# Attention backward: transposed softmax rows are made where they are used and moved inside SBUF, and ScalarE issues them and the dV stores

## The chip, the cores and the metric

The kernel runs on one core of one Trainium2 chip. The metric is the device time of one execution in microseconds, lower is better; the median over runs of the same kernel is compared.

## The reference, cut to what matters

One token goes through an adaLN block: attention against a cache of 32 heads x 8192 keys x 192, then a small gated mixer and MLP. The kernel returns the output and eight gradients. The bulk is the gradients of the two caches.

```
def _A_ref(x, k_cache, v_cache, wq, wo):          # B = Sq = 1, 32 heads, Sk = 8192, Dh = 192
    q = (x @ wq).reshape(B, Sq, Hq, Dh).transpose(0, 2, 1, 3)
    scores = einsum('bhqd,bhkd->bhqk', q, k) * Dh ** (-0.5)
    p = softmax(scores)
    o = einsum('bhqk,bhkd->bhqd', p, v)
    return o.transpose(...).reshape(B, Sq, Hq * Dh) @ wo
...
_out, _vjp = jax.vjp(_f, A_x, A_k_cache, A_v_cache, A_wq, A_wo, B_w3, B_w4, c, w_mod)
return (_out, *_vjp(grad_out))
```

With e = exp(score - max) and do the gradient at the attention output of a head, dV[k, :] = e[k] / sum(e) * do, an outer product, and dK[k, :] = ds[k] * q with ds made from V . do. So every byte of K and of V is read, V is read a second time, and every byte of dK and dV is written, all in bf16.

## The kernel before, in words

A head's 8192 keys lie as 128 partitions x 64 columns (J = 64); a half is 32 columns (JH), 1.5 MB of K or V. E_all keeps e of all heads, column j of head h at E_all[:, h, j].

**Forward** (lines 509 to 598, then an ending written out by hand for the last two heads). Per head, SyncE (SP) loads two halves of K and two of V. VectorE (DVE) multiplies K by q, TensorE (PE) sums over the 192 columns, ScalarE (ACT) takes exp, and PE accumulates three sums over the keys. For each pair of heads, e_rows transposes the pair's 128 columns of E_all on PE, e_rows_out copies the result from PSUM on ScalarE, and GpSimd (POOL) stores it to eT_d, a scratch tensor in DRAM (line 431). There are 16 such pairs.

**Middle.** The mixer, the MLP and their backward, on single columns: a long chain of small operations. From line 777 on the backward's pools are open. do_mm makes do of the last heads (ScalarE writes do_r at line 839), and load_er fetches the first two halves' rows of e.

**Backward** (lines 1234 to 1285). 64 stages, one per half head, last heads first. A stage s does this:

- DVE: pq = V * do in two quarters (mul_q, L936); PE sums it over the columns (tree_q, L945); DVE reduces (L313) and makes dS4 (L1242).
- DVE writes dK in two parts (dk_part, L961); POOL stores it (store, L1194).
- dV: eight groups of four PE matmuls of depth 1 (dv_groups, L956). A weight is one row of 128 values of e, taken from er_b, which has its rows on partitions 0, 32, 64 and 96. ScalarE copies each group from PSUM (L957). Two PSUM buffers (psV) and two er_b buffers are in turn. After the eighth group, POOL issues load_er for stage s + 2 (L801), then the store of dV (L1194).
- SP loads the V half of a later stage (L293).
- slot() puts in pieces of the weight gradients (g_do, g_dq, g_wm, g_dwo): they load wq, w_mod and wo, transpose them on PE and store dwq, dw_mod and dwo.

The order on PE, DVE, ScalarE and SP is the order in which the code writes the operations (manual_schedule with ORDER)[...]. V halves have three buffers. dV and dK take five buffers in turn (out_b): dV of stage s is number 2s, dK is 2s + 1, so dK of stage s overwrites what dV of stage s - 2 left, and dV of stage s what dK of stage s - 3 left.

dv() says how many dV groups stand at a place. The eighth of a stage stands at the end of the stage, before the second part of dK in the text of the program.

Of the kernel before, what the change touches and what calls it, by code (L numbers as in the profile page):

```python
# [8 lines left out]
FP32 = mybir.dt.float32  # L9
BF16 = mybir.dt.bfloat16  # L10
ALU = mybir.AluOpType
# [9 lines left out]
def kernel(  # L21
# [26 lines left out]
    nc = tc.nc  # L48
    P = 128
    D = A_x.shape[-1]  # L50
    _, HQ, S, DH = A_k_cache.shape
# [3 lines left out]
    J = S // P  # L55
    JH = J // 2
# [4 lines left out]
    NQ = QD // P  # L61
    NMB = NMOD // P
    NT = HQ // 2
# [3 lines left out]
    MW = DH + 1  # L67
# [5 lines left out]
    V_, A_, T_ = nc.vector, nc.scalar, nc.tensor  # L73

    const = ctx.enter_context(tc.tile_pool(name="const", bufs=1))
# [6 lines left out]
    psB = ctx.enter_context(tc.tile_pool(name="psB", bufs=1, space=PS))  # L82
    psS = ctx.enter_context(tc.tile_pool(name="psS", bufs=1, space=PS))

    ORDER = {mybir.EngineType.PE, mybir.EngineType.DVE, mybir.EngineType.Activation, mybir.EngineType.SP}
    dram = ctx.enter_context(tc.tile_pool(name="dram", bufs=1, space=bass.MemoryType.DRAM))


    A_.preload_act_table_set("natural_log_exp_and_others")
    ident_bf = const.tile([P, P], BF16, name="ident_bf")  # L90
# [21 lines left out]
    def col(n, name, dtype=FP32):  # L112
        return const.tile([P, n], dtype, name=name)
# [42 lines left out]
    def layernorm(x, name):  # L156
        res = []
        for _ in g_layernorm(x, name, res):
            pass
        return res[0]  # L160
# [41 lines left out]
    dV_hd = [out_3[0, h].rearrange("(p j) d -> p j d", p=P) for h in range(HQ)]  # L202
# [49 lines left out]
    n0, r0 = layernorm(x_c, "ln0")  # L252
# [18 lines left out]


    E_all = const.tile([P, HQ, J], BF16, name="E_all")
    M1 = const.tile([P, HQ, MW], FP32, name="M1")
    M2 = const.tile([P, NT, MW], FP32, name="M2")
    AO = const.tile([P, ND, HQ], FP32, name="AO")
    rinv = col(HQ, "rinv")
    o_col = col(NQ, "o_col")
# [33 lines left out]
    def dot_sum(ps, dst):  # L312
        V_.reduce_sum(out=dst, in_=ps, axis=AX.X)  # L313

    eT_d = dram.tile([HQ * J, P], BF16, name="eT_d")
    NKB = 5
    KB = [kp.tile([P, JH, DH], BF16, name=f"KB{b}") for b in range(NKB)]

# [1 line left out]
    H1 = HQ - 1  # L320
    TL = NT - 1
# [2 lines left out]
    OR = (KY, KC, KE, KX, KD)  # L324
    NVA = (7 * JQ) // 16
    MO = 256
    with tc.tile_pool(name="vs", bufs=3) as vsp, tc.tile_pool(name="ft", bufs=2) as ft, \
            tc.tile_pool(name="psM", bufs=2, space=PS) as psM, tc.tile_pool(name="psO", bufs=2, space=PS) as psO, \
            tc.tile_pool(name="psR", bufs=2, space=PS) as psR:
# [36 lines left out]
        def m_units(q, kb, vs, mp, last=3):  # L366
# [7 lines left out]
            def rest():  # L374
                for k in range(JQ):
                    p0 = 64 * (k % 2)
                    T_.matmul(mp[p0 : p0 + 64, MO : MO + MW], lhsT=kb[:, j0 + k, P:DH], rhs=vs[:, k, 0:MW], start=False, stop=(z and k >= JQ - 2), skip_group_check=True)  # L377

# [28 lines left out]
        def mp_out(h, mp):  # L407
            A_.copy(out=M1[:, h, :], in_=mp[:, 0:MW])
            mt = ft.tile([P, MW], FP32, name="mt", bufs=1)
            A_.copy(out=mt[64:128, :], in_=mp[64:128, MO : MO + MW])  # L410
            return mt
# [7 lines left out]
        def m_add(h, mp, mt):  # L419
            t, b = divmod(h, 2)  # L420
            V_.tensor_tensor(out=M2[64 * b : 64 * b + 64, t, :], in0=mp[0:64, MO : MO + MW], in1=mt[64:128, :], op=ALU.add)

        def e_rows(t, pool=psS, tag="s"):
            ps = pool.tile([P, P], BF16, name="er_ps", tag=tag)
            T_.transpose(out=ps[0 : 2 * J, :], in_=E_all[:, 2 * t : 2 * t + 2, :].rearrange("p h j -> p (h j)"), identity=ident_bf)
            return ps

        def e_rows_out(t, ps):
            er = ft.tile([P, P], BF16, name="er", bufs=1)
            A_.copy(out=er[0 : 2 * J, :], in_=ps[0 : 2 * J, :])  # L430
            nc.gpsimd.dma_start(out=eT_d[2 * t * J : (2 * t + 2) * J, :], in_=er[0 : 2 * J, :])

        def pair_sum(po, b, os_h):
            rows = slice(64 * b, 64 * b + 64)
            for k in range(3):
                T_.matmul(po[rows, k : k + 1], lhsT=os_h[:, k:DH:3], rhs=c32[:, 0:1], start=True, stop=True)
            T_.matmul(po[rows, 3:4], lhsT=c32[:, 0:64], rhs=os_h[:, DH:MW], start=True, stop=True)
            T_.matmul(po[:, 4 + b : 5 + b], lhsT=c32, rhs=os_h[:, DH:MW], start=True, stop=True)
# [27 lines left out]
        X, os_, wo_l = {0: {"k": [load_k(0, 0), load_k(0, 1)], "v": [load_v(0, 0, VB[0])]}}, {}, {}  # L466
        wo_l[0] = load_wo(0)
        wch = None
        V_.memset(M1[:, H1 - 1 : HQ, :], 0.0)
        V_.memset(M2[:, TL, :], 0.0)  # L470
        dgs = list(range(NF))
        w4v = B_w4.rearrange("(a p) r -> p a r", p=P)
        a1, nga, sS, sS2, C_S, S_m = col(ND, "a1"), col(ND, "nga"), col(ND, "sS"), col(ND, "sS2"), col(1, "C_S"), col(1, "S_m")
# [35 lines left out]
        with tc.manual_schedule(engines=ORDER):  # L509
            for i in range(H1):  # L510
# [5 lines left out]
                t = (i - 3) // 2  # L516
# [44 lines left out]
                    vs = scale_v(2, y["v"][1], E4, Ef)  # L561
                if last:
                    A_.copy(out=AO[:, :, 2 * t : 2 * t + 2], in_=pair_ao(o2, wo_l.pop(t)))
                    e_rows_out(t, e_rows(t))
                if i % 4 == 3 and wch is not None:
                    q_half((i + 1) // 4, 1, wch)
                    wch = None
# [77 lines left out]
            score_tree(1, d0)  # L645
            o_quarter(3, z["vs"], z["op"])
            mt = m_out(H1 - 2, z["mp"], z["op"], os_)
            e_rows_out(TL - 1, e_rows(TL - 1, psB, "b"))
            es = e_sum(H1 - 1)
            dg_part(1)  # L650
            op_y = psO.tile([P, 256], FP32, name="op")
# [43 lines left out]
            pair_sum(po, 1, os_.pop(H1 - 2))  # L695
            o2 = pair_o(TL - 1, po)
            pair_sum(po_x, 1, os_.pop(H1))
            e_rows_out(TL, e_rows(TL, psB, "b"))
            ps_ao = pair_ao(o2, wo_l[TL - 1])
            w3t(1)  # L700
            o2 = pair_o(TL, po_x)
# [13 lines left out]
            ps = mean_mm(x1, ND)  # L715
# [8 lines left out]
            ps = mean_mm(pr, 2 * ND)  # L724
# [9 lines left out]
            ps = mean_mm(pr, 2 * ND)  # L734
# [48 lines left out]
    cpr = col(HQ, "cpr")  # L783
    ckS = col(NQ, "ckS")
# [9 lines left out]
    NS = 2 * HQ  # L794

    def load_er(s):

        er = bst.tile([P, R8, P], BF16, name="er_b", bufs=2)
        h, t = ht(s)
        r0 = h * J + t * JH  # L800
        nc.gpsimd.dma_start(out=er[0:P:32, :, :].rearrange("r k p -> r (k p)"), in_=eT_d[r0 : r0 + JH, :].rearrange("(r k) p -> r (k p)", r=4))  # L801
        return er

    def ht(s):
# [115 lines left out]
    def late_rows():  # L920
        V_.tensor_tensor(out=bo, in0=h2_ps, in1=xc2, op=ALU.add)
        dw4_rows(flat(VB[0])[:, 2 * D :], 5, 7)
        dw4_store(flat(VB[0]), 3, 9)
        v_l[2] = load_v(*ht(2), VB[0])
        dw4_rows(stg0, 0, 3)
        dw4_store(stg0, 0, 3)
        hm = col(1, "hm")
        V_.tensor_scalar(out=hm, in0=vt[:, 1:2], scalar1=r1[:, 0:1], scalar2=S_m[:, 0:1], op0=ALU.mult, op1=ALU.add)
        V_.tensor_scalar(out=bo, in0=bo, scalar1=hm[:, 0:1], scalar2=None, op0=ALU.add)
        V_.tensor_tensor(out=ao, in0=aoP, in1=aoN, op=ALU.add)  # L930
        V_.memset(dha, 0.0)
        V_.memset(dsc, 0.0)
        V_.memset(dq_x, 0.0)

    def mul_q(s, q):
        V_.tensor_tensor(  # L936
# [121 lines left out]
    def g_dq(t):  # L1058
# [6 lines left out]
        else:  # L1065
            for lo, hi, M, b in ((0, P, M1[:, 2 * t, 0:DH], 0), (0, P, M1[:, 2 * t + 1, 0:DH], 2), (0, 64, M2[0:64, t, 0:DH], 1), (64, P, M2[64:128, t, 0:DH], 1)):
                h = 2 * t + (1 if (b == 2 or lo == 64) else 0)
# [19 lines left out]
    def g_small():  # L1087

        ck3 = ckS.rearrange("p (t b) -> p t b", b=3)
        for b, h0 in ((0, 0), (2, 1)):  # L1090
            V_.tensor_tensor(out=ck3[:, :, b], in0=M1[:, h0:HQ:2, DH], in1=cpr[:, h0:HQ:2], op=ALU.mult)
        for lo, hi, h0 in ((0, 64, 0), (64, P, 1)):
            V_.tensor_tensor(out=ck3[lo:hi, :, 1], in0=M2[lo:hi, :, DH], in1=cpr[lo:hi, h0:HQ:2], op=ALU.mult)
        A_.mul(out=ckS, in_=ckS, mul=SCALE)
        V_.tensor_tensor(out=d_cb, in0=d_sb, in1=n1, op=ALU.mult)
        V_.tensor_tensor(out=d_ga, in0=dx1, in1=ao, op=ALU.mult)
        yield
        V_.tensor_tensor(out=d_gb, in0=bo, in1=dy_c, op=ALU.mult)
        x2 = tcol(ND, "x2")
        V_.tensor_tensor(out=x2, in0=bo, in1=gb, op=ALU.mult)  # L1100
        V_.tensor_tensor(out=x2, in0=x2, in1=x1, op=ALU.add)
        store_vec(x2, out_0[0], "x2")
        yield
# [87 lines left out]

    def store(dst, s, src, lo=0, hi=JH):
        h, t = ht(s)
        nc.gpsimd.dma_start(out=dst[h][:, t * JH + lo : t * JH + hi, :], in_=src[:, lo:hi, :])  # L1194

    def dv_gen():
        for s in range(NS):
            dV, er, doh = out_b(2 * s), er_l.pop(s), do_of(ht(s)[0])
            for n, g in enumerate((0, 2, 4, 6, 1, 3, 5, 7)):
                dv_groups(dV, er, doh, (g,))  # L1200
                if n == 7:
                    if s + 2 < NS:
                        er_l[s + 2] = load_er(s + 2)
                    store(dV_hd, s, dV, JQ if s == 0 else 0, JH)
                elif n == 3 and s == 0:
                    store(dV_hd, s, dV, 0, JQ)
                yield
# [7 lines left out]
    ps = psR.tile([P, JH, TS], FP32, name="dot_ps")  # L1215
# [18 lines left out]
    for s in range(NS):  # L1234
        h, t = ht(s)
# [7 lines left out]
            out=dS4,  # L1243
            in0=dP[:, :, None].to_broadcast([P, JH, 4]),
            scalar=cpr[:, h : h + 1],
            in1=E_all[:, h, t * JH : (t + 1) * JH, None].to_broadcast([P, JH, 4]),
# [8 lines left out]
        if nxt:  # L1255
            ps = psR.tile([P, JH, TS], FP32, name="dot_ps")
# [59 lines left out]
```

## Time and profile before

| | |
|---|---|
| Median of 14 runs | 1445.3 us (1441.19 to 1454.22) |
| The profiled execution, its own time | 1450.06 us |
| Its span | 1448.3 us |
| Busy in the span: PE, DVE, ACT, POOL | 1186.0, 1111.2, 882.2, 143.6 us |
| Moved by DMA | 572.48 MB, 395 GB/s on the mean |
| DMA queue of SP (hardware) | 51402 packets, 343.59 MB, 59.1% of 16 engines |
| DMA queue of POOL (software) | 26704 packets, 226.97 MB, 37.9% |
| DMA queue of ScalarE (hardware) | 20 packets, 0.00 MB |
| Granted TensorE clock | 0.73 over the span, about 0.57 in the backward |

Busy time is that of the engine's own instructions; a DMA is issued by one engine and carried out by the 16 DMA engines, whose busy share is told per stretch of time. "A <- B" in a wait means that A stood idle until B was done. The profiled execution is 4.8 us above the median, so differences are worked out on the profile and then set against the median.

### The profile page before, as it was taken

To read this page: it belongs to the slowest core of one execution; us is meant where nothing else is said; L and a number is where in the kernel's file an instruction comes from. 1 tells how busy PE (TensorE), PEld (TensorE's weight loads), DVE (VectorE), ACT (ScalarE), POOL (GpSimd) and SP (SyncE) were. 2 spreads that over 40 slices of the span, in tenths; PEclk is the share of its full clock that TensorE was granted. 3 is DMA by queue.
4 is the path that set the end of the run, shared out by engine and by line. 5 is a ranking of instruction groups with operands and counts; after the bars stand their busy time and mean duration, and the time that the engine had idled before them with its cause. 6 is when DMAs were issued, how large, how long until landed. Compare 5 with 4: busy or idle time off the path is not lost.

```text
span 1448.3 us, 29985 instructions
## 1 busy us (share of the span) xinstructions
PE 1186.0 (82%) x12577; PEld 776.9 (54%) x12577; DVE 1111.2 (77%) x1396; ACT 882.2 (61%) x1923; POOL 143.6 (10%) x256
## 2 busy tenths in 40 slices
PE   3999999899999998777788777778788887677974
PEld 1677777677777677544444444444444444344532
DVE  5999999999999997577666666667766667677674
ACT  0777767777777773545556555656656565455654
POOL 0000000000000000112111111111111011011111
PEclk9999999999999997756555655565555556655555
DMA  9999999999999996599999999999999999999997
GB/s 375 399 408 417 414 418 402 399 403 402 398 392 397 414 387 259 206 361 426 423 426 418 416 396 392 420 417 401 402 418 415 418 419 412 390 379 416 419 408 330
DMA packets 78261, 572.48 MB, mean 395 GB/s; under 512 B 8846, under 2 KB 26974, under 8 KB 37806
## 3 DMA queue, kind: packets, MB, share of 16 engines
q1 hardware_dynamic: 51402, 343.59, 59.1%
q0 software_dynamic: 26704, 226.97, 37.9%
q8 instruction: 98, 1.61, 0.4%
q14 instruction: 37, 0.30, 0.1%
q10 hardware_dynamic: 20, 0.00, 0.0%
HBM read 344.10 MB, written 226.43 MB: 394 GB/s over the span
## 4 chain that ended last, share of the span: by engine, by line
PE 36%; DVE 27%; DMA 14%; ACT 11%; issue 10%; POOL 1%; SPq 0%; POOLq 0%; ACTq 0%; DVEq 0%
PE dot_ps L945 14%; DVE prod L298 8%; DMA out_dram<-KB 7%; DVE pq L936 5%; PE dv_ps L956 5%; ACT vs L357 4%; PE mp L372 3%; DVE prod L303 3%; DVE vs L350 3%; PE wT_ps L824 3%; PE dot_ps L309 3%; PE mp L377 2%; ACT wT L825 2%; ACT KB L957 2%; DMA KB<-in_A_k_cache_dram 2%
## 5 line engine op out<-in xcount | busy, mean ns | idle before, releaser
L957 ACT CAST KB<-dv_ps 128x768 bf16<-128x768 f32 x504 | 382.0, 804 | 284.9 <-PE dv_ps L956 284.0
L945 PE MATMUL dot_ps<-pq,ident_bf 128*128 128x256 bf16 x1536 | 355.1, 400 | 76.1 <-DVE pq L936 75.9
L357 ACT ACTIVATE vs<-VB,Ef 128x192 bf16<-128x192 bf16 x840 | 303.2, 443 | 0.0
L945 PEld LDWEIGHTS <-ident_bf 128*128 128x128 bf16 x1536 | 186.9, 132 | 199.3 <-issue 139.6
L956 PE MATMUL dv_ps<-do_r,er_b 1*128 1x192 bf16 x2048 | 215.8, 328 | 64.1 <-ACT KB L957 55.1
L961 DVE TENSOR_TENSOR KB<-qs_bc,dS 128x3072 bf16<-128x3072 bf16 x126 | 220.6, 1751 | 44.0 <-DMA out_dram<-KB 38.9
L936 DVE TENSOR_TENSOR pq<-VB,do_r 128x3072 bf16<-128x3072 bf16 x126 | 220.5, 1750 | 6.2 <-DMA VB<-in_A_v_cache_dram 6.2
L298 DVE TENSOR_TENSOR prod<-KB,qs_bc 128x6144 bf16<-128x6144 bf16 x62 | 207.8, 3352 | 13.0 <-DMA KB<-in_A_k_cache_dram 6.9
L956 PEld LDWEIGHTS <-er_b 1*128 1x128 bf16 x2048 | 90.2, 110 | 182.1 <-issue 170.0
L372 PE MATMUL mp<-vs,KB 128*128 128x193 bf16 x1920 | 187.7, 251 | 0.0
L372 PEld LDWEIGHTS <-KB 128*128 128x128 bf16 x1920 | 168.6, 100 | 18.7 <-issue 4.6
L313 DVE TENSOR_REDUCE dP<-dot_ps 128x32 f32<-128x512 f32 x64 | 44.2, 691 | 127.6 <-PE dot_ps L945 127.6
L309 PE MATMUL dot_ps<-prod,ident_bf 128*128 128x512 bf16 x372 | 94.4, 391 | 42.1 <-DVE prod L303 42.1
L350 DVE TENSOR_TENSOR vs<-VB,E 128x1728 bf16<-128x1728 bf16 x120 | 123.5, 1049 | 0.0
L303 DVE TENSOR_TENSOR prod<-prod 128x3072 bf16<-128x3072 bf16 x62 | 108.6, 1751 | 0.6
L825 ACT COPY wT<-wT_ps 128x1024 bf16<-128x1024 bf16 x84 | 80.8, 962 | 42.0 <-PE wT_ps L824 40.5
L377 PE MATMUL mp<-vs,KB 128*64 128x193 bf16 x1920 | 104.2, 252 | 0.0
L801 POOL DMA_DIRECT2D er_b<-eT_d x64 | 37.0, 579 | 600.5 <-PE dv_ps L956 574.5
L377 PEld LDWEIGHTS <-KB 128*64 128x64 bf16 x1920 | 77.9, 110 | 19.7 <-issue 19.7
L309 PEld LDWEIGHTS <-ident_bf 128*128 128x128 bf16 x372 | 34.6, 99 | 83.6 <-issue 55.7
L1194 POOL DMA_DIRECT2D out_dram<-KB x127 | 68.5, 544 | 35.4 <-ACT KB L957 29.9
L337 ACT ACTIVATE E<-S_h,negm 128x256 bf16<-128x256 f32 x30 | 15.2, 508 | 82.0 <-DVE negm L532 82.0
(335 smaller groups left out, 1018.2 us busy)
## 6 DMA issues: line engine op xcount, KB each, us to landing
VB<-in_A_v_cache_dram SPq DMA_DIRECT2D x125, 1536.0 KB, 11.8
out_dram<-KB POOLq DMA_DIRECT2D x125, 1536.0 KB, 16.0
KB<-in_A_k_cache_dram SPq DMA_DIRECT2D x64, 1536.0 KB, 10.2
wo_st<-in_A_wo_dram SPq DMA_DIRECT2D x30, 480.0 KB, 8.4
w_st<-in_A_wq_dram SPq DMA_DIRECT2D x12, 960.0 KB, 13.8
out_dram<-wo_st POOLq DMA_DIRECT2D x16, 480.0 KB, 20.4
out_dram<-w_st POOLq DMA_DIRECT2D x7, 960.0 KB, 21.1
w_st<-in_w_mod_dram SPq DMA_DIRECT2D x6, 960.0 KB, 21.9
```

Of the source, the lines that this page charges most:

```text
L298: V_.tensor_tensor(out=prod, in0=src, in1=vec[:, None, :].to_broadcast([P, JH, DH]), op=ALU.mult)
L303: V_.tensor_tensor(out=prod[:, :, 0:w], in0=prod[:, :, 0:w], in1=prod[:, :, w : 2 * w], op=ALU.add)
L309: T_.matmul(ps, lhsT=ident_bf, rhs=prod[:, :, k : k + TS], start=(k == 0), stop=(k == w - TS))
L350: V_.tensor_tensor(out=vs[:, 0:n, 0:DH].rearrange("p j (a b) -> p j a b", b=4), in0=v[:, v0 : v0 + n, :].rearrange("p j (a b) -> p j a b", ...
L357: A_.activation(out=vs[:, k, 0:DH], in_=v[:, v0 + k, :], func=ACT.Copy, scale=Ef[:, j0 + k : j0 + k + 1])
L372: T_.matmul(mp[:, 0:MW], lhsT=kb[:, j0 + k, 0:P], rhs=vs[:, k, 0:MW], start=(q == 0 and k == 0), stop=(z and k == JQ - 1), skip_group_chec ...
L377: T_.matmul(mp[p0 : p0 + 64, MO : MO + MW], lhsT=kb[:, j0 + k, P:DH], rhs=vs[:, k, 0:MW], start=False, stop=(z and k >= JQ - 2), skip_grou ...
L936: V_.tensor_tensor(out=pq[:, q], in0=v_l[s][:, q * JQ : (q + 1) * JQ, :], in1=do_of(ht(s)[0])[:, None, :].to_broadcast([P, JQ, DH]), op=AL ...
L945: T_.matmul(ps[:, q * JQ : (q + 1) * JQ, :], lhsT=ident_bf, rhs=pq[:, q, :, k : k + TS], start=(k == 0), stop=(k == DH - TS), skip_group_c ...
L956: T_.matmul(ps[:, b, k * DH : (k + 1) * DH], lhsT=er[p0 : p0 + 1, 2 * m + k, :], rhs=doh[p0 : p0 + 1, :], start=True, stop=True)
L957: A_.copy(out=dV4[:, 2 * q : 2 * q + 2, m * PW : (m + 1) * PW], in_=ps[:, :, 0:PW])
L961: V_.tensor_tensor(out=dK[:, lo:hi, :].rearrange("p j (a b) -> p j a b", b=4), in0=qh.rearrange("p (a b) -> p a b", b=4)[:, None, :, :].to ...
```

## The change

The scratch tensor in DRAM goes. The forward makes no transposed rows any more, except those of the last pair, which stay in SBUF in er_t. In the backward, at the end of stages 2, 6, 10 up to 58, PE transposes the next pair's columns and ScalarE copies them into er_t, 15 times. load_er moves 32 rows of 128 values from er_t to er_b, SBUF to SBUF, and ScalarE issues it; ScalarE also issues the stores of dV. POOL keeps the stores of dK and of the weight gradients. M1, M2 lose the parts of the last two heads, which held zeros, and ckS is cleared there instead.

```
-    dram = ctx.enter_context(tc.tile_pool(name="dram", bufs=1, space=bass.MemoryType.DRAM))
+    erp = ctx.enter_context(tc.tile_pool(name="erp", bufs=1))
...
-    M1 = const.tile([P, HQ, MW], FP32, name="M1")
-    M2 = const.tile([P, NT, MW], FP32, name="M2")
+    M1 = const.tile([P, HQ - 2, MW], FP32, name="M1")
+    M2 = const.tile([P, NT - 1, MW], FP32, name="M2")
...
-    eT_d = dram.tile([HQ * J, P], BF16, name="eT_d")
...
+    def e_rows(t, pool=psS, tag="s"):
+        ps = pool.tile([P, P], BF16, name="er_ps", tag=tag)
+        T_.transpose(out=ps[0 : 2 * J, :], in_=E_all[:, 2 * t : 2 * t + 2, :].rearrange("p h j -> p (h j)"), identity=ident_bf)
+        er = erp.tile([P, P], BF16, name="er_t")
+        A_.copy(out=er[0 : 2 * J, :], in_=ps[0 : 2 * J, :])
+        return er
...
-        def e_rows_out(t, ps):
-            er = ft.tile([P, P], BF16, name="er", bufs=1)
-            A_.copy(out=er[0 : 2 * J, :], in_=ps[0 : 2 * J, :])
-            nc.gpsimd.dma_start(out=eT_d[2 * t * J : (2 * t + 2) * J, :], in_=er[0 : 2 * J, :])
...
-                    e_rows_out(t, e_rows(t))
...
-            e_rows_out(TL - 1, e_rows(TL - 1, psB, "b"))
...
-            e_rows_out(TL, e_rows(TL, psB, "b"))
+            er_t = [e_rows(TL, psB, "b")]
...
         er = bst.tile([P, R8, P], BF16, name="er_b", bufs=2)
         h, t = ht(s)
-        r0 = h * J + t * JH
-        nc.gpsimd.dma_start(out=er[0:P:32, :, :].rearrange("r k p -> r (k p)"), in_=eT_d[r0 : r0 + JH, :].rearrange("(r k) p -> r (k p)", r=4))
+        r0 = (h % 2) * J + t * JH
+        nc.scalar.dma_start(out=er[0:P:32, :, :], in_=er_t[0][r0 : r0 + JH, :])
         return er
...
     def store(dst, s, src, lo=0, hi=JH):
         h, t = ht(s)
-        nc.gpsimd.dma_start(out=dst[h][:, t * JH + lo : t * JH + hi, :], in_=src[:, lo:hi, :])
+        (nc.scalar if dst is dV_hd else nc.gpsimd).dma_start(out=dst[h][:, t * JH + lo : t * JH + hi, :], in_=src[:, lo:hi, :])
...
                 if n == 7:
+                    if s % 4 == 2 and s + 2 < NS:
+                        er_t[0] = e_rows(TL - s // 4 - 1)
                     if s + 2 < NS:
                         er_l[s + 2] = load_er(s + 2)
                     store(dV_hd, s, dV, JQ if s == 0 else 0, JH)
```

In the built program the order of every engine is otherwise the same. POOL issues 145 fewer DMAs (16 stores to eT_d, 64 loads of er_b, 65 stores of dV), and ScalarE 129 more.

More of the change, by code (lines that the diff above doesn't have):

```diff
@@ L421, in m_add @@
             V_.tensor_tensor(out=M2[64 * b : 64 * b + 64, t, :], in0=mp[0:64, MO : MO + MW], in1=mt[64:128, :], op=ALU.add)
[L423 to L426, printed above, removed]
-        def e_rows_out(t, ps):
-            er = ft.tile([P, P], BF16, name="er", bufs=1)
-            A_.copy(out=er[0 : 2 * J, :], in_=ps[0 : 2 * J, :])
-            nc.gpsimd.dma_start(out=eT_d[2 * t * J : (2 * t + 2) * J, :], in_=er[0 : 2 * J, :])
         def pair_sum(po, b, os_h):
@@ L468 @@
         wch = None
-        V_.memset(M1[:, H1 - 1 : HQ, :], 0.0)
-        V_.memset(M2[:, TL, :], 0.0)
         dgs = list(range(NF))
@@ L933, in late_rows @@
         V_.memset(dq_x, 0.0)
+        V_.memset(ckS[:, 3 * TL : NQ], 0.0)
     def mul_q(s, q):
@@ L1090, in g_small @@
         for b, h0 in ((0, 0), (2, 1)):
-            V_.tensor_tensor(out=ck3[:, :, b], in0=M1[:, h0:HQ:2, DH], in1=cpr[:, h0:HQ:2], op=ALU.mult)
+            V_.tensor_tensor(out=ck3[:, 0:TL, b], in0=M1[:, h0 : H1 - 1 : 2, DH], in1=cpr[:, h0 : H1 - 1 : 2], op=ALU.mult)
         for lo, hi, h0 in ((0, 64, 0), (64, P, 1)):
-            V_.tensor_tensor(out=ck3[lo:hi, :, 1], in0=M2[lo:hi, :, DH], in1=cpr[lo:hi, h0:HQ:2], op=ALU.mult)
+            V_.tensor_tensor(out=ck3[lo:hi, 0:TL, 1], in0=M2[lo:hi, :, DH], in1=cpr[lo:hi, h0 : H1 - 1 : 2], op=ALU.mult)
         A_.mul(out=ckS, in_=ckS, mul=SCALE)
```

## The prediction

> **What bounds the kernel now.** I read the page's slices first, then busy time by stretches, then the waits from 640 us on, then single tiles and the timeline at both ends of the backward.
>
> ```profile
> DMA  9999999999999996599999999999999999999997
> 20.00:560.00 540.00, 491.60 (x7031) 376.01 (x7034) 504.68 (x481) 376.89 (x1194) 8.26 (x15) 0.97 1.00 404
> 560.00:604.00 44.00, 33.13 (x497) 26.18 (x486) 31.70 (x118) 21.81 (x38) 6.01 (x9) 0.65 0.36 126
> 644.00:1396.00 752.00, 595.47 (x4509) 338.06 (x4508) 517.35 (x731) 436.57 (x616) 114.95 (x200) 0.57 1.00 411
> 1412.00:1432.00 20.00, 16.62 (x114) 8.43 (x113) 15.83 (x13) 12.99 (x18) 2.71 (x5) 0.50 0.78 324
> ```
>
> The columns are length, busy time of PE, PE loads, DVE, ACT and POOL, clock, DMA share, GB/s. The DMA engines are full, 1.00, in the forward and from 644 to 1396 us, while the busiest engine there, PE, has 79%. Only the middle (0.36) and the end (0.78) leave room: 28 us and 4 us. So time is won or lost in the middle, at the end, and by what changes the DMA engines' own work. A stall of an engine in the full stretch costs only what exceeds the cover. I size that cover from stages 59 to 61, where side work is over and loads are ending: POOL's er_b issues follow each other after 10.1 and 10.3 us, against 13.3 us a stage on the mean (55 stages from 667.7 to 1397.9 us). The side work's DVE rows (TENSOR_SCALAR of L1083, L1047 and L1051, reductions of L1069) come to about 1.5 us a stage and PE's (L824, L838, L1045) hold the trees up by about as much, not always at the same time; I take 1 us a stage to spare, a choice.
>
> ```profile
> POOL er_b L801 <- PE dv_ps L956: 567.7, 59, 17.8
> ACT KB L957 <- PE dv_ps L956: 272.8, 217, 5.5
> PE dv_ps L956 <- ACT KB L957: 54.4, 84, 1.5
> DVE KB L961 <- DMA out_dram<-KB: 38.9, 18, 8.8
> POOL out_dram L1194 <- ACT KB L957: 29.2, 58, 8.8
> PEld L956 <- DMA er_b<-eT_d: 9.0, 6, 4.2
> PE dv_ps L956 <- DMA er_b<-eT_d: 6.7, 3, 4.0
> ```
>
> Waits on transfers that the change touches: 38.9 us for stored buffers, 15.7 us for er_b. They end sooner after the change, but with the DMA engines full the time then shows as another wait for the same bytes.
>
> [...]
>
> **The change, part by part.**
>
> *Forward.* Out go 15 transposes and copies (217 and 267 ns, beside DMA) and 15 stores of 32 KB. Each is 16 packets of 2048 B[...], of 82 ns on the mean of POOL's packets of that size class: 15 x 0.08 = **-1.2 us** where DMA is full. Bounds -3 (the transposes also wait 3.6 us) and 0. The memsets and the shorter ckS products (under 1 us) lie beside the loads at the start and in the side work: 0; without that cover under 1 us.
>
> *Middle.* POOL issued the first two er_b loads at 580.6 and 581.2 and they landed at 584.4, well before PE needs them:
>
> ```profile
> 580.59 1.14 POOL L801 DMA_DIRECT2D er_b<-eT_d  x2 [16.32 <-PE w3T_ps L674]
> 587.88 0.42 ACT L839 ACTIVATE do_r<-do_ps,rinv 128x192 bf16<-128x192 f32 x1 [1.29 <-PE do_ps L838]
> 589.03 0.50 PE L956 MATMUL dv_ps<-do_r,er_b 1*128 1x192 bf16 x4
> ```
>
> On ScalarE they stand after L839, so they issue at about 588.3 and 588.7 (0.33 to 0.55 us each, SP's and ScalarE's rows). The quickest landing from the trace is 3 us (ScalarE's 1.36 us issue at the start of the kernel frees PE at 4.36): er_b is there at 591, and the first dv matmul moves from 589.0 by 2. Behind it in PE's order stand c_ps and the first tree, so the whole chain to the V load at 603.7 moves: **+1.9 us**, DMA being idle there. Bounds 0 (a shorter copy within SBUF) and +4.
>
> *Full stretch, DMA.* Bytes stay: 0.5 MB written and 0.5 MB read leave, 0.5 MB inside SBUF comes. The form changes. Each er_b load was 4 packets of 2048 B, 82 ns[...]. 256 B packets took 17 ns on ScalarE's queue at the start[...]. I take **+5 us**[...]. Bounds 0 and +9. The dV stores keep their 12288 B packets, most at 460 ns on both queues: 0, bounds -4 and +4.
>
> *Full stretch, engines.* ScalarE gains, per stage, two issues of 0.33 us and the wait for its own last copy, some 0.9 us, and every fourth stage a copy of 0.27 us behind a transpose of 0.22 us. Behind these stand the next stage's first copies; PE has two psV buffers, and a group takes PE 1.0 to 1.4 us against 0.8 us of copy, so PE goes on. Covered by the 1 us and by ScalarE's idle 42%; without cover 0.9 x 58 = 52 us. POOL no longer holds dK's store behind er_b and dV. A new wait comes with the queue[...]. I set the landings, where the trace tells them, against the POOL issues that ScalarE takes over: most waits have 8 to 25 us to spare, seven have under 3, four of them are late by 0.4 to 3.4 us, all on or behind a load of wq, w_mod or wo. Such loads are slow already:
>
> ```profile
> L985 SPq DMA_DIRECT2D stg<-in_A_wq_dram x4: 379/412/1171, 700.0 to 1198.6; - x4
> DMA to landing us min/median/max: 3.8/19.3/34.7
> ```
>
> [...] seven waits of 2 to 8 us, about 35 us in ScalarE, of which psV hides 2 to 3 us each. The rest fits the spare microsecond a stage; I take **+2 us**, bounds 0 and +15. The V halves keep their distance: 10 to 20 us before use in most stages, 2.2 and 2.6 at the least. [...] The copy into er_t waits for the last load from it, one stage old and landed after 8.5 us in the median (17.5 at the most, before): 0, up to +4 once where it is late, inside the +15.
>
> *End.* dK's store now leaves when DVE is done, not behind dV on POOL:
>
> ```profile
> 1423.55 1.75 DVE L961 TENSOR_TENSOR KB<-qs_bc,dS 128x3072 bf16<-128x3072 bf16 x1
> 1429.20 1.06 POOL L1194 DMA_DIRECT2D out_dram<-KB  x2 [8.80 <-ACT KB L957]
> 1434.98 1.06 POOL L1194 DMA_DIRECT2D out_dram<-KB  x2 [4.72 <-ACT KB L957]
> ```
>
> dK of stage 62 is ready at 1425.3 and leaves after 1429.7, while the DMA engines idle 22% of 20 us. Filling that saves up to 4.4 us; ScalarE's issues lengthen three uncovered stages by up to 0.6 us each. **-2.5 us**, bounds -4 and +1.
>
> Sum: -1.2 + 1.9 + 5 + 2 - 2.5 = +5.2 us. On the profiled 1450.06 that is 1455.3; on the median, 4.8 us lower, **1450.5**.
>
> **Rivals.** *Faster.* [...] the er_b copy lands within 1 us, the sum is -1.2 + 0 + 0 + 0 - 4 = -5: 1440. For it: dK's earlier store is sure, and er_b and dV each have a quieter queue. [...] *Much slower.* [...] 20 waits instead of seven, 5 us each, less 60 us of cover, plus V halves that come late: +15 to +25, 1460 to 1470. For it: 34.7 us for a load of wq[...]. [...] *Nothing to see.* DMA full before and after, ends cancel: 1445.
>
> **How the numbers follow.** A measurement of this kernel can tell about 0.2%, 3 us. My case (+1 to +10) gets 0.5, of which 0.15 fall within 0.2%; much slower 0.2; faster 0.2; nothing to see 0.1. That gives faster 0.20, same 0.25, slower 0.55. The range leaves out half of the faster case below -6 and the top of the slow one: 1439 to 1466; my case alone is 1446 to 1455.
>
> **What would show it.** Right: DMA share still 1.00 from 644 to 1396 us with GB/s a little lower (about 407); the first dv matmul later by 2 us against L839; dK's stores issued by POOL 3 us before dV's; waits for er_b near zero. A column of ScalarE waits on DMA, or DVE waits on V loads beyond 20 us, makes it the slow rival. Wrong: the full stretch shorter by 5 us or more, which would mean that the DMA engines were not the bound there.

## The result, and the profile after

The median went from 1444.8 us (48 runs) to 1467.93 us (10 runs, 1461.25 to 1472.21): ratio 1.0151, 95% interval 1.0131 to 1.0171, that is +21.8 us (18.9 to 24.7). The forecast was slower, at 1450.5; the time lies just above its range, 1439 to 1466.

The DMA row of the 40 slices on the changed kernel's page, and after it the busy times by stretches, with the columns used for the kernel before:

```profile
DMA  9999999999999994699999999999999999999997
```

```profile
20.00:560.00 540.00, 492.06 (x6988) 375.71 (x6987) 503.39 (x480) 372.75 (x1178) 0.00 (x0) 0.95 1.00 404
560.00:604.00 44.00, 32.53 (x453) 24.98 (x452) 29.27 (x118) 19.05 (x34) 1.96 (x2) 0.56 0.33 117
644.00:1396.00 752.00, 596.52 (x4454) 338.42 (x4452) 504.11 (x717) 432.79 (x619) 51.72 (x87) 0.55 1.00 403
```

The forward is as it was, 404 GB/s. The loss lies in the full stretch, from 644 to 1396 us: the DMA share still reads 1.00, but the engines move 403 GB/s instead of 411. The starts of DVE's reduction into dP, one per stage, tell where. Against before, stage 3 starts 4.1 us late, stage 60 23.6 us late, and the span ends 19.6 us late. So 19.5 us are lost over 57 stages, unevenly (the lag is 14.8 us at stage 16, 15.5 at stage 30, 20 at stage 39), and 4.0 us come back at the end. These are two single executions. What comes back at the end holds in the other runs too: from stage 60 on, the changed kernel, e2, e4, e6, e10 and e11, whose whole dV stores have left POOL, gain 2.5 to 4.8 us on the kernel before, and of those with them on POOL (e1, e3, e7, e9, e12) none gains more than 0.1 us.

The waits of the changed kernel from 640 us on (total us, times, longest):

```profile
ACT KB L950 <- PE dv_ps L949: 259.6, 233, 4.1
PE dv_ps L949 <- ACT KB L950: 77.3, 84, 2.7
DVE w_st L1040 <- ACT v_bc L1033: 42.4, 14, 5.0
DVE stg L1040 <- ACT v_bc L1033: 28.2, 12, 4.8
DVE KB L954 <- DMA out_dram<-KB: 19.4, 6, 4.2
ACT wT L817 <- DMA er_b<-er_t: 5.5, 13, 0.5
ACT KB L950 <- DMA er_b<-er_t: 1.9, 4, 0.5
POOL out_dram L1187 <- DVE KB L954: 208.3, 22, 15.5
```

Waits on transfers went down (DVE's for stored buffers from 38.9 to 19.4 us, PE's for er_b from 9.0 to nothing; the 15.7 us of the prediction count three waits twice, at a weight load and at the matmul behind it). Waits on ScalarE went up: PE for dV copies from 54.4 to 77.3, and DVE for v_bc, ScalarE's copy that feeds the rows of a weight gradient, from 50.5 to 70.6. The two lines of before:

```profile
DVE w_st L1047 <- ACT v_bc L1040: 30.1, 13, 3.9
DVE stg L1047 <- ACT v_bc L1040: 20.4, 11, 4.0
```

ScalarE itself hardly waits for DMAs (5.5 and 1.9 us above). POOL, with the dV stores gone, waits for DVE's dK (208.3 us) and stores it at once.

The end of stage 29, in the order of time, on ScalarE (ACTq is its sequencer, which issues the DMAs) in the changed kernel, from the timeline:

```profile
1017.56 0.80 ACT L950 CAST KB<-dv_ps 128x768 bf16<-128x768 f32 x1 [1.03 <-PE dv_ps L949]
1017.62 0.54 ACTq L793 DMA_DIRECT2D er_b<-er_t  x1
1018.39 0.44 ACTq L1187 DMA_DIRECT2D out_dram<-KB  x1
1019.00 2.20 ACT L950 CAST KB<-dv_ps 128x768 bf16<-128x768 f32 x3 [0.65 <-PE dv_ps L949]
```

In the kernel before, the same four copies follow each other without idle time, in one line of the view:

```profile
1001.93 2.93 ACT L957 CAST KB<-dv_ps 128x768 bf16<-128x768 f32 x4 [0.90 <-PE dv_ps L956]
```

This is the reading on which the rest turns. The er_b issue, 0.54 us, runs while the last dV copy computes. The dV store reads what that copy writes, so it is issued only at the copy's end (at 1018.39, the end being 1018.36; of the 65 dV stores none is issued earlier than 0.03 us after such an end), and ScalarE's next instruction starts 0.65 us after that end. I call this the **gap** and take its mean over stages 4 to 59, passing over the copy into er_t (and, below, unused copies): 0.82 us in the changed kernel, 0.11 in the kernel before. It can hold a wait for data too, so it is an upper mark, and the view names PE as what ended these 0.65 us. But no gap of these stages is under 0.40 us in the changed kernel, whatever follows, while the median before is -0.08 (the next copy starts just before the last one ends). Not every stage has more of it: at nine of them it was 0.37 us before already, with a wait for PE.

### The profile page after: what moved, and what is told of

Same layout as the page of the kernel before. It is cut to its first block, busy times and chain, and to the rows that moved or that the text cites. A ratio compares the mean times of both kernels' runs of the same rounds, so it can differ in the third digit from the quotient of the medians.

```text
span 1467.9 us, 29883 instructions
## 1 busy us (share of the span) xinstructions
PE 1210.8 (82%) x12577; PEld 788.1 (54%) x12577; DVE 1109.2 (76%) x1395; ACT 884.7 (60%) x1923; POOL 62.7 (4%) x111
## 3 DMA queue, kind: packets, MB, share of 16 engines
q8 instruction: 98, 1.61, 0.4%
## 4 chain that ended last, share of the span: by engine, by line
PE 45%; DVE 26%; ACT 14%; DMA 7%; issue 5%; ACTq 2%; SPq 0%; POOL 0%; DVEq 0%; POOLq 0%
PE dot_ps L938 21%; PE dv_ps L949 8%; DVE prod L297 8%; ACT vs L363 5%; ACT KB L950 4%; DVE pq L929 4%; DVE prod L302 3%; DVE vs L356 3%; PE mp L378 3%; PE wT_ps L816 3%; DMA KB<-in_A_k_cache_dram 2%; DMA out_dram<-KB 2%; PE dot_ps L308 2%; DVE S_h L312 2%; PE mp L383 2%
## 5 line engine op out<-in xcount | busy, mean ns | idle before, releaser
L938 PE MATMUL dot_ps<-pq,ident_bf 128*128 128x256 bf16 x1536 | 365.6, 409 | 44.8 <-DVE pq L929 44.7
L949 PE MATMUL dv_ps<-do_r,er_b 1*128 1x192 bf16 x2048 | 224.2, 340 | 79.5 <-ACT KB L950 77.3
L938 PEld LDWEIGHTS <-ident_bf 128*128 128x128 bf16 x1536 | 189.7, 135 | 174.4 <-issue 111.3
L954 DVE TENSOR_TENSOR KB<-qs_bc,dS 128x3072 bf16<-128x3072 bf16 x126 | 220.5, 1750 | 19.5 <-DMA out_dram<-KB 19.4
L949 PEld LDWEIGHTS <-er_b 1*128 1x128 bf16 x2048 | 93.6, 113 | 200.6 <-issue 196.6
L308 PEld LDWEIGHTS <-ident_bf 128*128 128x128 bf16 x372 | 34.9, 99 | 86.9 <-issue 59.3
L343 ACT ACTIVATE E<-S_h,negm 128x256 bf16<-128x256 f32 x30 | 15.2, 508 | 85.7 <-DVE negm L526 85.7
L395 PE MATMUL op<-vs,ones_bf 128*32 128x193 bf16 x1920 | 62.7, 251 | 0.0
L1187 POOL DMA_DIRECT2D out_dram<-KB x64 | 34.9, 545 | 599.1 <-DVE KB L954 218.8
```

The costliest lines, as they stand in the source:

```text
L308: T_.matmul(ps, lhsT=ident_bf, rhs=prod[:, :, k : k + TS], start=(k == 0), stop=(k == w - TS))
L938: T_.matmul(ps[:, q * JQ : (q + 1) * JQ, :], lhsT=ident_bf, rhs=pq[:, q, :, k : k + TS], start=(k == 0), stop=(k == DH - TS), skip_group_c ...
L949: T_.matmul(ps[:, b, k * DH : (k + 1) * DH], lhsT=er[p0 : p0 + 1, 2 * m + k, :], rhs=doh[p0 : p0 + 1, :], start=True, stop=True)
L954: V_.tensor_tensor(out=dK[:, lo:hi, :].rearrange("p j (a b) -> p j a b", b=4), in0=qh.rearrange("p (a b) -> p a b", b=4)[:, None, :, :].to ...
```

## The experiments

Loss means time against the kernel before, run beside each on the same chip; a bracket behind a ratio or a loss is its 95% interval. Theory A is ScalarE's time at the stage's end, B the third queue with large packets, C the 256-byte packets of the er_b loads; D is in the third expectation text.

**1 to 4: each half of the change alone.** In the changed kernel, or in the kernel before:

```
e1: store():    (nc.scalar if dst is dV_hd else nc.gpsimd)  ->  nc.gpsimd
e2: load_er():  nc.scalar  ->  nc.gpsimd
e3: both of these
e4: kernel before, store():  nc.gpsimd  ->  (nc.scalar if dst is dV_hd else nc.gpsimd)
```

> The changed kernel with one part undone: the dV stores are issued by POOL again, the er_b loads stay on ScalarE. The changed kernel lost 23 us against the kernel before (1467.9 against 1444.8). Theory A, ScalarE's own time: each stage ScalarE issues two DMAs (0.54 us for er_b, 0.34 us for dV) and waits for its own last copy, and this time pushes the next dV copies back, PE's dv matmuls with them, and the next tree. Undoing the dV store takes away its 0.34 us and the wait for the copy, so about half of the loss comes back: +8 to +14 us over before, and DVE's waits on the tree (161.9 us after, 127.6 before) fall by half. Theory B, the third queue: [...] nearly all comes back (+0 to +5), since the queue keeps only 256-byte packets. Theory C[...]: nothing comes back (+18 to +24).

Measured: ratio 0.9995 (0.9979 to 1.0012), -0.7 us (-3.0 to +1.7).

> The changed kernel with the other part undone: the er_b loads (still from er_t in SBUF) are issued by POOL, the dV stores stay on ScalarE. Theory A (ScalarE's own time): 0.54 us of the two issues a stage goes, about half comes back or somewhat more: +6 to +14 us over before. Theory B (the third queue with the dV stores): nothing comes back, +18 to +24. Theory C [...] most comes back: 0 to +6.

Measured: 1.0131 (1.0089 to 1.0174), +18.9 us.

> The changed kernel with er_b loads and dV stores both on POOL: what stays of the change is that the rows of e stay in SBUF and are made in the backward. Theories A, B and C all say that the loss is gone: -4 to +3 us against before. If the loss comes from the 15 transposes and copies in the backward, or from the load waiting for them (theory D), it stays: +15 or more.

Measured: 1.0008 (0.9985 to 1.0031), +1.2 us.

> The kernel before with one part of the change: ScalarE issues the dV stores; eT_d and POOL's er_b loads stay. Theory A: one issue of 0.34 us and a wait for its own copy each stage, less than half of the cost of the change: +5 to +12 us. Theory B: the third queue with large packets is there: +15 to +24. Theory C or D: 0, or faster by 2 to 4 us since dK's stores no longer stand behind dV's.

Measured: 1.0086 (1.0057 to 1.0116), +12.4 us (8.2 to 16.7).

The dV stores on ScalarE are the loss. The er_b loads on ScalarE, their packets of 256 bytes and the transposes in the backward cost nothing that shows (e1 has all three, at -0.7 us), so C and D fall. A's guess that the two issues share the loss was wrong. B foresaw e1 and e2 better than A did, and e4 lies between the two; what parts them is whether the dV stores cost as DMAs or as ScalarE's time.

**5 and 8: the stores cut by partitions.**

```
e5: dV[112:128] by nc.scalar, dV[0:112] by nc.gpsimd
e8: dV[0:64] and dV[64:128], both by nc.scalar
```

> The changed kernel with each dV store split: partitions 112 to 127 (an eighth of the bytes) are stored by ScalarE at the place of the old store, the rest by POOL. The runs so far say that the dV stores on ScalarE cost some 18 us and the er_b loads nothing. Theory A, ScalarE's own time: in the trace the er_b issue (0.54 us) runs while the last copy of the stage still computes, but the dV store must wait for that copy and is issued after it (0.34 us), so ScalarE's next copy starts some 0.4 us late in each stage. The eighth needs the same wait and an issue of its own: +13 to +20 us over before. Theory B, the third queue [...] it has an eighth of them: 0 to +3.

Measured: 1.1246 (1.1207 to 1.1285), +180 us.

> The changed kernel with each dV store of ScalarE cut in two issues, partitions 0 to 63 and 64 to 127; bytes, packets and their queue stay. Theory A: another 0.34 us of ScalarE a stage at the same place, over some 58 stages up to 20 us more than the changed kernel: +33 to +43 over before. Theory B: as the changed kernel, +19 to +26.

Measured: 1.1499 (1.1456 to 1.1543), +216 us.

Neither theory said anything like it. The issues by themselves became long; the first line is of e5, the second of e8, from their lines on ScalarE (ns min/median/max):

```profile
L1188 ACTq DMA_DIRECT2D out_dram<-KB x63: 321/812/3227, 624.5 to 1605.7; - x63
```

```profile
L1189 ACTq DMA_DIRECT2D out_dram<-KB x126: 473/1126/4519, 625.1 to 1648.0; - x126
```

The gap became 2.28 and 3.83 us. The stores' packets of 12288 bytes also took 695 and 693 ns on the mean on ScalarE's queue, against 462 when all partitions are stored at once; the median is 460 in all three, so a part of the packets became very long (a tenth took over 1.2 us). The two cannot be taken apart here, so these runs decide nothing between A and B. They say only that cutting this store by partitions cost far more than it could have brought.

**6: the same DMAs, the store issued later.**

```
 dv_groups(dV, er, doh, (g,))
+if n == 0 and held:
+    store(dV_hd, *held.pop())
...
-store(dV_hd, s, dV, JQ if s == 0 else 0, JH)
+held.append((s, dV, JQ if s == 0 else 0, JH))
+if s == NS - 1:
+    store(dV_hd, *held.pop())
```

> The changed kernel, but ScalarE issues the dV store of a stage only after it has been given the first dV copy of the next stage: the wait for the stage's own last copy is then over, and the issue of 0.34 us runs beside that first copy. Queues, packets and bytes are those of the changed kernel. Theory A: nearly all of the loss comes back, -3 to +5 us against before. Theory B: nothing comes back, +16 to +24, as the three queues are there as before.

Measured: 1.0033 (1.0017 to 1.0049), +4.8 us (2.5 to 7.1). Three queues, the same bytes, and 17 of the 21.8 us are back. The end, where this kernel too gains some 2.5 us, hides a part of what is left: B can own about 10 us of the full stretch at the most (7.1 + 2.5). The gap is 0.35 us. The later stores may have a share in what remains, since DVE waits longer for stored buffers in e6 than in e1 (the two lines are from the waits from 640 to 1400 us of e6 and of e1):

```profile
DVE KB L954 <- DMA out_dram<-KB: 39.1, 17, 6.4
```

```profile
DVE KB L954 <- DMA out_dram<-KB: 11.3, 7, 3.5
```

But the kernel before waits as long for them (37.6 us in that stretch), so this isn't shown.

**7 and 9: ScalarE's time without any DMA.** In e1, after the place of the store:

```
+A_.copy(out=erp.tile([P, 256], BF16, name="junk"), in_=qs_bc[:, 0:256])     # e9: twice
```

> The kernel with the dV stores on POOL (which takes as long as before), and at the old place of the store ScalarE makes a copy that nobody uses, 128x256 bf16 within SBUF, an estimated 0.4 us from the 0.24 us of 128x64 and the 0.48 us of 128x384. The copy moves no DMA. Theory A: that time at that place is what costs: +13 to +22 us over before. Theory B: DMA queues are as in the kernel that loses nothing: within 3 us of before.

Measured: 1.0026 (1.0008 to 1.0045), +3.8 us (1.2 to 6.5): below what A expected, and close to what B did. The copy takes 0.40 us, but the gap grew only from 0.31 to 0.48 us: a copy starts about 0.1 us before the one ahead of it ends (in e9's timeline below at 1008.82, against 1008.93; the next text says 0.2), and a part of this one fills idle time that e1 has there in any case (the median gap is 0.22 us in both). So the dose was made larger.

> The kernel with the dV stores on POOL and, at the old place of the store, two of the unused copies in ScalarE instead of one. In the trace of the run with one, a dummy takes 0.40 us but starts 0.2 us before the end of the copy ahead of it, so that ScalarE's next useful instruction starts 0.48 us after the stage's last copy on the mean, against 0.31 without it and 0.82 in the changed kernel: it was a third of the dose. Two dummies bring it to some 0.85, the changed kernel's own delay, without any DMA. Theory A (ScalarE's time at that place): +12 to +23 us over before. Theory B (a third queue, or the time at which the store starts): +0 to +6, as with one.

Measured: 1.0148 (1.0113 to 1.0183), +21.4 us (16.3 to 26.5): as much as the changed kernel loses, at about its gap (0.90 us), with the queues of a kernel that loses nothing. The end of stage 29 in e9, the two unused copies in one line:

```profile
1008.13 0.80 ACT L950 CAST KB<-dv_ps 128x768 bf16<-128x768 f32 x1 [1.03 <-PE dv_ps L949]
1008.13 0.54 ACTq L793 DMA_DIRECT2D er_b<-er_t  x1
1008.82 0.84 ACT L1201 COPY junk<-qs_bc 128x256 bf16<-128x256 bf16 x2
```

The same stretch in e1 and then in e9:

```profile
644.00:1396.00 752.00, 605.45 (x4521) 343.71 (x4521) 515.64 (x723) 440.82 (x628) 82.86 (x145) 0.55 1.01 413
```

```profile
644.00:1396.00 752.00, 589.00 (x4452) 335.48 (x4452) 506.37 (x723) 470.08 (x730) 80.82 (x142) 0.57 1.00 405
```

Only ScalarE has more to do (470 for 441 us), every other engine gets less done, the DMA share stays at 1.00, and the rate falls by 8 GB/s. A DMA share of 1.00 therefore doesn't show here that the DMA engines set the time: at 1.00 they moved 405 GB/s in e9 and at 1.01 413 in e1, so they were busy longer for each byte. (SP's packets of 12288 bytes took 496 ns on the mean in e1, 506 in e9, 511 in the changed kernel, with a median of 460 in all three; but 481 in the kernel before, so their mean doesn't follow the loss.) The clock is out as well: 0.55 in the quicker, 0.57 in the slower. The waits of e9, from 640 to 1400 us, name the changed kernel's sufferers (e1: 51.4, 34.7, 26.5 us):

```profile
PE dv_ps L949 <- ACT KB L950: 65.2, 68, 2.1
DVE w_st L1040 <- ACT v_bc L1033: 42.8, 14, 5.2
DVE stg L1040 <- ACT v_bc L1033: 30.4, 12, 5.4
```

In its total, e9 loses what the changed kernel loses. In the profiles, from stage 3 to stage 60, it is 14.9 us against 19.5 (e1 1.0, e6 3.8), for e9 gains nothing at the end. So ScalarE's time explains the greater part of the loss; whether it explains the last 4 us or so, single executions can't tell. And no run put the unused copies at another place of the stage: that the place matters rests on e6.

**11: the order of the two issues exchanged.** In the changed kernel, the store stands ahead of load_er.

> The changed kernel with its two issues in the other order: first the dV store, then the er_b load. The same DMAs from the same queues. The dV store must wait for the last copy, and the er_b issue of 0.54 us, which ran beside that copy, now stands behind it. Theory A: ScalarE's next instruction starts 1.0 to 1.3 us after the last copy instead of 0.82, and at the 43 us per us that the changed kernel shows (21.8 us for 0.51 us more than without its dV stores) the loss grows to +28 to +43 us over before. Theory B: as the changed kernel, +18 to +25.

Measured: 1.061 (1.0572 to 1.0647), +88 us: more than either theory said. The gap was 1.82 us on the mean and 1.10 in the median. ScalarE's timeline shows the step that A named, both issues now behind the copy:

```profile
912.37 0.80 ACT L950 CAST KB<-dv_ps 128x768 bf16<-128x768 f32 x1 [1.03 <-PE dv_ps L949]
913.20 0.34 ACTq L1187 DMA_DIRECT2D out_dram<-KB  x1
913.63 0.54 ACTq L793 DMA_DIRECT2D er_b<-er_t  x1
914.22 1.01 ACT L817 COPY wT<-wT_ps 128x1024 bf16<-128x1024 bf16 x1 [1.05 <-PE bc_t L1024]
```

The waits from 640 to 1500 us show what it had left out, the small load now standing on the queue behind 1.5 MB of store:

```profile
PE dv_ps L949 <- DMA er_b<-er_t: 57.4, 13, 6.7
```

Less those 57 us, which may not all lie on the path, some 31 are left, within A's 28 to 43. That split is a sum, not a run.

**10: SP issues the dV stores** (nc.sync in store(), er_b on ScalarE).

> The changed kernel with the dV stores issued by SP, in whose order each stands ahead of the next V load; er_b stays on ScalarE. SP waits 660 us for free V buffers, so its own time costs nothing, but a V load now starts behind a wait for the stage's last dV copy, and loads and stores share a queue. Theory A: ScalarE is free again, -3 to +5 us against before, provided that V loads 1 to 3 us later still come in time. Theory B[...]: +10 or more.

Measured: 1.0083 (1.0062 to 1.0105), +12.0 us (9.0 to 15.2): outside A's range and within B's. DVE waits for no V half. From the waits from 640 to 1400 us, it is the loads of wo that stand behind the stores:

```profile
PE wT_ps L816 <- DMA wo_st<-in_A_wo_dram: 18.4, 3, 14.8
PE dv_ps L949 <- ACT KB L950: 47.5, 68, 1.3
```

ScalarE's part is gone (47.5 us), and the order on SP's queue took its place: against the kernel before, e10 is 3.9 us ahead at stage 5, in which PE waits 14.8 us for wo, 11.2 us behind at stage 6, and 13.0 behind at stage 60.

**12: a version from these findings.** e1 with two er_t buffers, the transposes made after the fourth dV group:

```
-erp = ctx.enter_context(tc.tile_pool(name="erp", bufs=1))
+erp = ctx.enter_context(tc.tile_pool(name="erp", bufs=2))
...
+if n == 3 and s % 4 == 2 and s + 2 < NS:
+    er_n.append(e_rows(TL - s // 4 - 1))
 if n == 7:
     if s % 4 == 2 and s + 2 < NS:
-        er_t[0] = e_rows(TL - s // 4 - 1)
+        er_t[0] = er_n.pop()
```

> A version meant to beat both kernels: dV stores on POOL and er_b loads on ScalarE, as in the run that took as long as before, but the new rows er_t are made after the fourth dV group of stages 2, 6, 10 and so on instead of after the eighth, into a second er_t buffer. In the changed kernel's order the er_b issue of these 15 stages waits for the copy into er_t, so that ScalarE's next instruction starts some 0.8 us after the last dV copy there; now all er_b issues run beside the last copy. Theory A: 15 stages with 0.6 to 0.8 us less at the place that costs, at the 0.45 to 0.75 us of time for each us that the runs with one dummy and the changed kernel show, 4 to 8 us, less the 0.27 us of the copy, which now stands elsewhere (up to 4 us): -7 to 0 against before. Theory B says nothing of it: as without, within 2 us of before.

Measured: 1.0008 (0.9984 to 1.0033), +1.2 us. The gap fell from 0.31 to 0.14 us as meant, and the time did not follow. Set side by side:

| kernel | gap, us | loss, us (95% interval) |
|---|---|---|
| before | 0.11 | 0 |
| e12 | 0.14 | +1.2 (-2.3 to +4.8) |
| e3 | 0.20 | +1.2 (-2.2 to +4.5) |
| e1 | 0.31 | -0.7 (-3.0 to +1.7) |
| e6 | 0.35 | +4.8 (2.5 to 7.1) |
| e7 | 0.48 | +3.8 (1.2 to 6.5) |
| e4 | 0.54 | +12.4 (8.2 to 16.7) |
| e2 | 0.68 | +18.9 (12.9 to 25.1) |
| changed | 0.82 | +21.8 (18.9 to 24.7) |
| e9 | 0.90 | +21.4 (16.3 to 26.5) |

(e5, e8 and e11, with larger gaps, stand above. e10 had 0.62, of which 0.27 is the one wait for wo; its median is e1's, 0.22. In e2 and e4 PE also waited 17.8 and 21.2 us for er_b that POOL had issued late, and e6 has the later stores. The rows that differ in ScalarE's time alone are e1, e7 and e9.) Up to a gap of about 0.3 us ScalarE's delay is hidden; between 0.3 and 0.8 us, half a microsecond in each of some 57 stages (28 us) goes with about 20 us.

## Why the prediction was wrong in size

- **Full stretch, engines, +2: the step that failed.** It said that two issues and the wait for ScalarE's own copy, some 0.9 us, were "covered by the 1 us and by ScalarE's idle 42%". The gap grew by 0.71 us, near enough, but the cover (what a stage can lose without the kernel taking longer) is some 0.2 us a stage (a gap of 0.31 instead of 0.11 costs nothing), not 1 us. The spare microsecond came from comparing mean stages with the shortest ones and holding the difference to be slack behind full DMA engines; e9 shows that it is no such slack. ScalarE's idle time is no cover either: it waits for PE in it (259.6 us), in other places of the stage. What stands behind the last dV copy on ScalarE is on the chain in many stages: copies that empty PE's buffers, and the wT, vrow and v_bc copies that end in a wait of DVE. That reading comes from the waits; that the time at this place costs is what e9 and e6 show. Mis-sized by some 18 us: about 20 instead of 2, above the term's own bound of +15. The new waits of ScalarE, some 35 us in the working, were my estimate and aren't there: the 17 waits of ScalarE that the view puts down to DMAs are of 0.5 us at the most, 7.4 us in all (5.5 + 1.9), and the long ones that were foreseen are missing.
- **The two issues are not alike.** The working counted them as one sum. The one that needs nothing from the last copy costs nothing that shows (e1, -0.7 us); the one that waits for it does (e2, +18.9 us). The store's issue also took 0.50 us on the mean in the changed kernel, where it stands behind the er_b issue (median 0.34, longest 1.61), and at most 0.34 in e11, where the 1.5 MB stores stand ahead of it.
- **Full stretch, DMA, +5: not there.** The packets are small (a load has 32 of 256 bytes, at 18 ns on the mean in the changed kernel), but e1 has them all and loses nothing (-0.7 us). The +5 was my estimate; how the packets lie on the DMA engines was not shown. The step also took for granted that the DMA engines set the end. The sign named for the opposite, a shorter stretch, could not have shown it: the stretch grew, through another engine.
- **Middle, +1.9: +0.7.** The first dv matmul comes 1.88 us after the start of the do_r copy instead of 1.15. The 3 us assumed for the landing was too long: in the changed kernel's timeline PE starts 1.87 us after the issue:

```profile
588.42 0.42 ACT L831 ACTIVATE do_r<-do_ps,rinv 128x192 bf16<-128x192 f32 x1 [1.29 <-PE do_ps L830]
588.43 1.23 ACTq L793 DMA_DIRECT2D er_b<-er_t  x2
590.30 0.50 PE L949 MATMUL dv_ps<-do_r,er_b 1*128 1x192 bf16 x4 [0.66 <-DMA er_b<-er_t]
```

The rest of the 4.1 us at stage 3 stays unexplained: single executions with the same forward differ by more there, and e1 stands 9.5 us ahead of before. So the forward's -1.2 can't be judged either.
- **End, -2.5: -4.0.** The size lies at its bound, and the first half of the mechanism was right: dK's stores leave when DVE is done with them, so that dK of the last stage no longer leaves after dV. POOL's two last stores and ScalarE's last in the changed kernel's timeline (before, POOL issued dV and dK of the last stage one behind the other from 1434.98 on):

```profile
1449.88 0.53 POOL L1187 DMA_DIRECT2D out_dram<-KB  x1 [10.28 <-DVE KB L954]
...
1457.74 0.53 POOL L1187 DMA_DIRECT2D out_dram<-KB  x1 [7.33 <-DVE KB L954]
...
1460.33 0.34 ACTq L1187 DMA_DIRECT2D out_dram<-KB  x1
```

The span ends 7.5 us after the start of the last issue; before, 12.8 us after it (1435.5). The second half was not: the DMA engines didn't become fuller in the last stages, as the prediction put it: their share over the 30 us before the engines stop is 0.85 before and 0.80 after.

- **The slow rival had the number (1460 to 1470) and not the mechanism.** It needed ScalarE to stand in long waits behind SP's loads, and such waits are missing (none of ScalarE's on a DMA is longer than 0.5 us). Its sum, as written, doesn't come out either: 20 waits of 5 us less 60 us of cover are 40 us, not 15 to 25. The faster rival took er_b to be free of cost, which e1 bears out, yet it had left out ScalarE.
- **That "slower" came true is luck.** Of the +5.2 us, +6.9 stood on the middle and on er_b's packets, which gave 0.7 and nothing that shows; the term that made the kernel slower was held to be nearly covered.

Open: what lengthens issues and packets of a store cut by partitions (cut so, it was tried only on ScalarE's queue), how e6's 4.8 us divide between late stores and the third queue, and how much of the changed kernel's loss, beyond ScalarE's time, the third queue owns.

## What to carry to other kernels

In the changed kernel, a DMA that ScalarE issued from data of its own last instruction cost the wait for that instruction's end and the issue, 0.40 us or more ahead of all that follows (0.82 on the mean); an issue of 0.54 us that needs nothing from it ran beside it. Before you move an issue to a busy engine, look on the timeline at what that engine does next and who waits for it, not at its idle share. And a DMA share of 1.00 was no proof that transfers set the time (e9 lost 21.4 us at it, with no DMA added): put some idle work on an engine at the disputed place, and see whether the time moves.

## What the runs showed that I had not expected

- Stored in one piece (128 partitions, the changed kernel), 1.5 MB took ScalarE 0.34 us in the median to issue and 462 ns on the mean for a packet of 12288 bytes; in two pieces of 64 partitions (e8), 1.13 us in the median for each issue, and 693 ns on the mean for a packet.
- An 8 KB load behind a 1.5 MB store on the same queue (e11) kept PE waiting 57.4 us in all, 6.7 us at the most; ahead of it, in the changed kernel, PE waits for none from 640 us on.
- What an added instruction costs isn't its own length: one unused ScalarE copy of 0.40 us added 0.17 us to the gap (e7), and the second, which starts only when the first is done (0.84 us for the two in e9), 0.42 us.
